# AV of both heads of a pair in one step of 32 matmuls over two PSUM banks, the heads alternating matmul by matmul

## Chip, cores, metric

One core of one Trainium2 chip. The metric is the device time of one launch in microseconds. A profiled run also has a span, from its first to its last instruction, about 2 us shorter. Every run called fast here is of the usual state; the two single looks are of state "unknown" (one run each) and are used for their traces.

## The reference, cut to what matters

```
q, k, v: 8 batches x 12 heads x 448 x 64
scores = (q/|q|) @ (k/|k|).T / tau;  attn = softmax(scores);  o = attn @ v      # AV
x = o as 3584 x 768;  out = ((x @ w1) * (x @ w2)) @ w3 @ w_out                  # the FFN
```

The kernel takes heads in 48 pairs. For a pair: normalise q and k (GpSimd, VectorE), transpose them (L308), scores (L326), exp (ScalarE), AV (L340), divide by the row sums (VectorE, "normalisation"), transpose back (L362). Six pairs make a batch; only then can the FFN matmuls of that batch run (L375, groups of 6 x 189 ns or 8 x 162 ns).

## The kernel before: the parts that matter

AV has one step per head. A group of four matmuls (c = 0..3) adds into 65 columns, 64 of v and one of ones, whose column is the row sum:

```python
def av(pp, hh):
    ps = full(f"av{pp}.{hh}")[:, :NJ * (D + 1)].rearrange("p (m d) -> p m d", m=NJ)   # one bank
    for m, q0 in enumerate(QT):
        for c in range(NJ):
            nc.tensor.matmul(ps[:, m, :], exps[pp][:, c, hh, q0:q0 + 128],   # weights
                             vt[:, 2 * i + hh, c, :],                        # moving, 65 columns
                             start=(c == 0), stop=(c == NJ - 1))
v_tiles = [wpool.tile([P, GH, NJ, D + 1], BF16, ...)]                        # rows of 130 bytes
```

The order of all instructions is not written down; a planner inside the kernel makes it when the program is built. It holds a book of when each engine is free and each bank is given back, from durations that it is told. TensorE takes the step of lowest rank among those that can start within 0.15 us of the earliest; attention comes before the FFN.

```python
HOP = 0.25                                             # from one engine to another
tol = 0.15 if eng == "PE" else 0.05
add(f"sc{nb}", ...)                                    # 3 chunks: needs all six banks 0..5
add(f"av{p}.{h}", [("PE", 0.525)], ..., banks=SHORT)   # any one of banks 0..5
add(f"an{p}.{h}", [("DVE", 0.62)], ..., [f"av{p}.{h}"], reads=[(f"av{p}.{h}", None)])  # gives it back
fill(f"a{b}.{fo}", 1.137, ...)                         # an FFN group, banks 7, 6, ...
```

What the planner makes is fixed on the chip: every engine works in that order and waits where something is late.

## Time and profile before

| | before |
|---|---|
| time, median of 2 | 393.09 us (392.95 to 393.23) |
| TensorE busy in the 298 us from 45 to 343 | 297.83 us |
| one AV block of 32, from its first start to the next instruction's | 1,029 ns |
| AV of the last pair starts | 341.3 us |
| after the last transposes back: FFN alone | 43 us |

How to read it: TensorE is busy without a gap, so the number of its nanoseconds is the time. The last row is the cushion of FFN work that attention can be late by; the prediction works out what of it is free. Starts are taken from the single records of the trace; the profile merges them.

### The profile page before, as it was taken

How to read it: one execution, taken by the hardware profiler on the slowest of the kernel's cores; microseconds unless marked ns; L12 is line 12 of the kernel's file. 1: busy time of each engine (PE TensorE's matmuls, PEld its weight loads, DVE VectorE, ACT ScalarE, POOL GpSimd, SP SyncE). 2: the span in 40 equal slices, each digit the busy share in tenths (PEclk: the TensorE clock that was granted, in tenths of full speed). 3: DMA queues.
4: the chain of work that ended last, by engine and by line, in shares of the span. 5: the costliest groups of instructions: out<-in, count | busy, mean ns of one | idle time of the engine just before them, and what ended most of it. 6: DMA issues, size and time to landing. Idle time of an engine off the chain costs nothing.

```text
span 391.0 us, 9650 instructions
## 1 busy us (share of the span) xinstructions
PE 382.9 (98%) x4012; PEld 231.1 (59%) x4012; DVE 215.5 (55%) x495; ACT 243.9 (62%) x401; POOL 243.8 (62%) x256
## 2 busy tenths in 40 slices
PE   8899999999999999999999999999999999999995
PEld 4578665565655666565655565555656566555553
DVE  5798745686737668557568657543534434330210
ACT  4998768456765766766765767746566666613222
POOL 8598998999999989999999999713400000000000
PEclk9999999999999999999999999999999999999999
DMA  8999999627476484828437194301200032004005
GB/s 142 199 203 200 210 208 195 82 35 134 96 91 86 79 149 80 108 32 145 85 45 103 26 143 105 35 2 42 82 2 3 3 88 75 2 2 121 0 10 153
DMA packets 43691, 35.18 MB, mean 90 GB/s; under 512 B 3968, under 2 KB 37632, under 8 KB 43648
## 3 DMA queue, kind: packets, MB, share of 16 engines
q0 software_dynamic: 38368, 23.11, 42.8%
q1 hardware_dynamic: 4784, 11.07, 9.7%
q8 instruction: 31, 0.51, 0.5%
q10 hardware_dynamic: 496, 0.40, 0.3%
q14 instruction: 12, 0.10, 0.1%
HBM read 46.66 MB, written 11.01 MB: 148 GB/s over the span
## 4 chain that ended last, share of the span: by engine, by line
PE 69%; POOL 21%; DMA 5%; issue 3%; DVE 1%; POOLq 0%; DVEq 0%
PE ps L375 47%; POOL nrm L289 9%; PE ps L340 9%; POOL sq L255 8%; PE ps L326 7%; DMA wo_sb<-in_moe_w_out_dram 4%; PE ps L308 3%; PE ps L362 2%; POOL raw L224 2%; POOL v_sb L240 2%; DMA raw<-in_k_dram 2%; DVE nrm L289 1%; DVE osd L353 0%; PE ps L388 0%; POOL vraw L231 0%
## 5 line engine op out<-in xcount | busy, mean ns | idle before, releaser
L331 ACT ACTIVATE expT<-ps 112x896 bf16<-112x896 f32 x192 | 166.1, 922 | 24.8 <-PE ps L326 24.6
L375 PE MATMUL ps<-xT,w_sb 128*128 128x448 bf16 x768 | 161.2, 353 | 0.0
L375 PEld LDWEIGHTS <-w_sb 128*128 128x128 bf16 x768 | 69.1, 98 | 66.1 <-issue 13.0
L289 POOL TENSOR_TENSOR nrm<-raw,rn 112x512 bf16<-112x512 bf16 x88 | 89.0, 1037 | 11.3 <-PE ps L308 10.0
L255 POOL TENSOR_TENSOR sq<-raw 112x512 bf16<-112x512 bf16 x85 | 86.0, 1040 | 0.7 <-DMA raw<-in_q_dram 0.5
L375 PE MATMUL ps<-w_sb,abT 128*128 128x384 bf16 (+2 forms) x456 | 80.0, 323 | 0.0
L421 DVE TENSOR_TENSOR abT<-a_sb,ps 128x448 bf16<-128x448 bf16 x64 | 39.7, 620 | 67.3 <-PE ps L375 64.3
L410 ACT CAST a_sb<-ps 128x448 bf16<-128x448 f32 x64 | 34.1, 534 | 58.3 <-PE ps L375 58.3
L261 DVE TENSOR_REDUCE ss<-sq 112x8 f32<-112x512 bf16 x96 | 62.9, 679 | 12.3 <-POOL sq L255 11.9
L375 PEld LDWEIGHTS <-abT 128*128 128x128 bf16 x456 | 41.7, 98 | 31.5 <-issue 7.0
L340 PEld LDWEIGHTS <-expT 112*128 112x128 bf16 x1536 | 54.9, 98 | 6.7 <-issue 1.0
L340 PE MATMUL ps<-v_sb,expT 112*128 112x65 bf16 x1536 | 57.7, 194 | 0.2 <-ACT expT L331 0.2
L326 PE MATMUL ps<-qkT 64*128 64x448 bf16 x384 | 48.5, 353 | 0.2 <-DVE osd L353 0.2
L381 ACT COPY out_sb<-ps 128x384 f32<-128x384 f32 (+1 forms) x43 | 20.5, 477 | 43.7 <-PE ps L375 40.4
L353 DVE TENSOR_TENSOR osd<-ps,rs 128x256 bf16<-128x256 f32 x96 | 40.8, 425 | 3.3
L316 DVE COPY qkT<-ps 128x896 bf16<-128x896 bf16 x48 | 29.6, 618 | 9.9 <-PE ps L308 9.9
L369 DVE COPY xT<-ps 128x448 bf16<-128x448 bf16 x48 | 18.6, 387 | 28.5 <-PE ps L362 23.1
L240 POOL COPY v_sb<-vraw 112x1536 bf16<-112x1536 bf16 x16 | 23.4, 1462 | 15.4 <-PE ps L340 12.0
L326 PEld LDWEIGHTS <-qkT 64*128 64x128 bf16 x384 | 13.4, 94 | 27.0 <-issue 20.7
L308 PE MATMUL ps<-ident,nrm 112*128 112x112 bf16 x384 | 26.9, 213 | 0.6 <-ACT expT L331 0.3
L383 DVE COPY out_sb<-ps 128x384 f32<-128x384 f32 (+1 forms) x14 | 7.5, 538 | 33.9 <-PE ps L375 33.9
L375 PE MATMUL ps<-wo_sb,w3t_sb 128*128 128x192 bf16 (+1 forms) x192 | 23.8, 273 | 1.2 <-DMA wo_sb<-in_moe_w_out_dram 1.2
(38 smaller groups left out, 208.8 us busy)
## 6 DMA issues: line engine op xcount, KB each, us to landing
vraw<-in_v_dram POOLq DMA_DIRECT2D x16, 336.0 KB, 5.6
raw<-in_q_dram POOLq DMA_DIRECT2D x15, 336.0 KB, 5.7
raw<-in_k_dram POOLq DMA_DIRECT2D x15, 336.0 KB, 7.6
w_sb<-in_moe_w_dram POOLq DMA_DIRECT2D x2, 1536.0 KB, 24.8
out_dram<-out_sb SPq DMA_DIRECT2D x7, 336.0 KB, 3.7
out_dram<-out_sb SPq DMA_DIRECT2D x8, 288.0 KB, 3.2
out_dram<-out_sb SPq DMA_DIRECT2D x8, 240.0 KB, 2.6
w_sb<-in_moe_w_dram POOLq DMA_DIRECT2D x3, 512.0 KB, 15.4
```

Of the source, the lines that this page charges most:

```text
L240: nc.gpsimd.tensor_copy(v_tiles[g % NV][:, :, :, :D], vraws.pop(g))
L255: eng.tensor_mul(o, x, x)
L261: nc.vector.reduce_sum(sss[g][:, t, 2 * i:2 * i + 2, :], sqs.pop((g, i, t)), axis=AX.X)
L289: eng.tensor_mul(nrms[g][:, i, t].rearrange("p j h d -> p h j d"), raw_of(g, t, i), rns[g][:, t, 2 * i:2 * i + 2].to_broadcast([P, 2, NJ, D]))
L308: nc.tensor.transpose(ps[:, 1 - t, j * P:(j + 1) * P], n[:, i, t, j].rearrange("p h d -> p (h d)"), ident[:P, :P])
L326: nc.tensor.matmul(sc[:, hh, :S], kq[:, c * P:c * P + 128], kq[:, S:], start=True, stop=True)
L331: nc.scalar.activation(exps[pp][:, c], scs.pop((pp, c))[:P, :, :S], ACT.Exp, scale=1.0 / float(tau))
L340: nc.tensor.matmul(ps[:, m, :], exps[pp][:, c, hh, q0:q0 + 128], vt[:, 2 * i + hh, c, :], start=(c == 0), stop=(c == NJ - 1))
L353: nc.vector.tensor_mul(osds[pp][:, :, hh, :], ps[:, :, :D], rs.to_broadcast([128, NJ, D]))
L375: nc.tensor.matmul(o, l, r, start=(i == 0), stop=(i == len(pairs) - 1))
L410: nc.scalar.copy(a_sbs[b, fo], pms.pop(("a", b, fo))[:, :S])
L421: nc.vector.tensor_mul(abts[b // 2][:, fo, c0:c0 + S], a_sbs.pop((b, fo)), pms.pop(("b", b, fo))[:, :S])
```

## The change

Its intent: matmuls that follow each other no longer add into the same bank. For that each head has a bank of its own, and the two steps become one.

```diff
-    def av(pp, hh):
+    def av(pp):
-        ps = full(f"av{pp}.{hh}")[...]
+        ps = [ps_all[:, b, :NJ * (D + 1)]... for b in plan.bank[f"av{pp}"]]
         for m, q0 in enumerate(QT):
             for c in range(NJ):
-                nc.tensor.matmul(ps[:, m, :], exps[pp][:, c, hh, ...], vt[:, 2 * i + hh, c, :], ...)
+                for hh in range(2):
+                    nc.tensor.matmul(ps[hh][:, m, :], exps[pp][:, c, hh, ...], vt[:, 2 * i + hh, c, :], ...)
...
+        add(f"av{p}", [("PE", 1.05)], ..., banks=[(n, n + 1) for n in range(0, 6, 2)])
         for h in range(2):
-            add(f"av{p}.{h}", [("PE", 0.525)], ..., banks=SHORT)
-            add(f"an{p}.{h}", [("DVE", 0.62)], ..., [f"av{p}.{h}"], reads=[(f"av{p}.{h}", None)])
+            add(f"an{p}.{h}", [("DVE", 0.62)], ..., [f"av{p}"], reads=[(f"av{p}", slice(h, h + 1))])
```

More of the change, by code (lines that the diff above doesn't have):

```diff
@@ L332, in exp @@
                              scale=1.0 / float(tau))
-    def av(pp, hh):
+    def av(pp):
         g, i = divmod(pp, GP)
         vt = v_tiles[g % NV]
-        ps = full(f"av{pp}.{hh}")[:, :NJ * (D + 1)].rearrange("p (m d) -> p m d", m=NJ)
+        ps = [ps_all[:, b, :NJ * (D + 1)].rearrange("p (m d) -> p m d", m=NJ)
+              for b in plan.bank[f"av{pp}"]]
         for m, q0 in enumerate(QT):
             for c in range(NJ):
-                nc.tensor.matmul(
-                    ps[:, m, :],
-                    exps[pp][:, c, hh, q0:q0 + 128],
-                    vt[:, 2 * i + hh, c, :],
-                    start=(c == 0), stop=(c == NJ - 1))
-        if hh == 0:
-            osds[pp] = head_pool.tile([128, NJ, 2, D], BF16, tag="osd", name="osd")
-        pav[pp, hh] = ps
+                for hh in range(2):
+                    nc.tensor.matmul(
+                        ps[hh][:, m, :],
+                        exps[pp][:, c, hh, q0:q0 + 128],
+                        vt[:, 2 * i + hh, c, :],
+                        start=(c == 0), stop=(c == NJ - 1))
+        osds[pp] = head_pool.tile([128, NJ, 2, D], BF16, tag="osd", name="osd")
+        for hh in range(2):
+            pav[pp, hh] = ps[hh]
     def av_norm(pp, hh):
@@ L621 @@
             reads=[(f"tr{p}", None)])
+        add(f"av{p}", [("PE", 1.05)], p, lambda e, p=p: av(p),
+            [f"exp{p}.{c}" for c in range(NJ)] + [f"spread{g}"] + ([f"av{p - 1}"] if last else []),
+            [("osd", ("osd", p))], [("exp", p), ("vt", g)],
+            banks=[(n, n + 1) for n in range(0, 6, 2)])
         for h in range(2):
-            add(f"av{p}.{h}", [("PE", 0.525)], p + 0.5 * h, lambda e, p=p, h=h: av(p, h),
-                [f"exp{p}.{c}" for c in range(NJ)] + [f"spread{g}"]
-                + ([f"av{p}.0"] if h else [f"av{p - 1}.1"] if last else []),
-                [] if h else [("osd", ("osd", p))], [("exp", p), ("vt", g)], banks=SHORT)
             add(f"an{p}.{h}", [("DVE", 0.62)], p + 0.5 * h - 0.5,
-                lambda e, p=p, h=h: av_norm(p, h), [f"av{p}.{h}"], reads=[(f"av{p}.{h}", None)])
+                lambda e, p=p, h=h: av_norm(p, h), [f"av{p}"],
+                reads=[(f"av{p}", slice(h, h + 1))])
         add(f"tb{p}", [("PE", 0.235)], p + 1, lambda e, p=p: trback(p),
```

## The prediction

> **What bounds the kernel now.** I read the page first: the busy row, the slices, the chain that ended last, and the rows of matmuls.
>
> ```profile
> PE 382.9 (98%) x4012; PEld 231.1 (59%) x4012; DVE 215.5 (55%) x495; ACT 243.9 (62%) x401; POOL 243.8 (62%) x256
> ...
> PE   8899999999999999999999999999999999999995
> ...
> POOL 8598998999999989999999999713400000000000
> PEclk9999999999999999999999999999999999999999
> ...
> L375 PE MATMUL ps<-xT,w_sb 128*128 128x448 bf16 x768 | 161.2, 353 | 0.0
> ...
> L340 PEld LDWEIGHTS <-expT 112*128 112x128 bf16 x1536 | 54.9, 98 | 6.7 <-issue 1.0
> L340 PE MATMUL ps<-v_sb,expT 112*128 112x65 bf16 x1536 | 57.7, 194 | 0.2 <-ACT expT L331 0.2
> ```
>
> TensorE has no gap from the third slice on, at full clock. L340 is AV. Its mean of 194 ns is a latency, not a cost: matmuls overlap, so the cost is the distance from one start to the next. To be sure that busy means moving, I then read the waits of TensorE alone:
>
> ```profile
> PE ps L475 <- DVE warm_sb L469: 1.3, 1, 1.3
> PE ps L375 <- DMA wo_sb<-in_moe_w_out_dram: 1.2, 2, 0.9
> PE ps L388 <- DMA w_sb<-in_moe_w_dram: 0.7, 1, 0.7
> PE ps L308 <- ACT expT L331: 0.3, 1, 0.3
> PE ps L308 <- DVE nrm L289: 0.3, 1, 0.3
> PE ps L326 <- DVE osd L353: 0.2, 1, 0.2
> PE ps L340 <- ACT expT L331: 0.2, 1, 0.2
> ```
>
> In all 4.2 us, nearly all in the first 45. The chain of waits goes through GpSimd from about 110 to 200 us, but it joins TensorE over one 0.2 us wait (L326), and the order of times shows why that is no second bound: the last normalised q and k of pair 20 ends at 120.9 us and its transposes start at 142.8, 22 us later; for pair 8 the lead is 4 us, for pair 41 53 us. So after some 80 us GpSimd is ahead, and what is saved on TensorE shows in the end, as long as it has something to do. Last, the order of time around one AV step:
>
> ```profile
> 227.65 0.39 PE L362 MATMUL ps<-ident,osd 128*128 128x128 bf16 x4
> 227.81 1.11 PEld L340 LDWEIGHTS <-expT 112*128 112x128 bf16 x32
> ...
> 227.87 1.19 PE L340 MATMUL ps<-v_sb,expT 112*128 112x65 bf16 x32
> ...
> 228.83 0.42 DVE L353 TENSOR_TENSOR osd<-ps,rs 128x256 bf16<-128x256 f32 x1
> ...
> 228.90 0.56 PE L308 MATMUL ps<-ident,nrm 112*128 112x112 bf16 x8
> ```
>
> Both heads already run as one block of 32 (46 of the 48 pairs do), from 227.87 to the next start at 228.90: 1.03 us. Head 0 is normalised while head 1 is still multiplied. So grouping two steps into one gains nothing by itself; what is new is the order inside.
>
> **What the skill says.** The Trainium skill, "TensorE: Matmul & The Clock Gate", section "Back-to-back issue gap", gives N/2.4 + 2.5 ns between starts at full clock. The trace agrees for long matmuls: 448 columns 189 ns (186.7 + 2.5), 112 columns 49 ns (49.2), 128 columns 56 ns (55.8). For AV's 65 columns it gives 29.6 ns; the trace has mostly 32 to 34. No page says what an accumulation into just-written elements costs. "PSUM — Partial Sum Buffer", section "The four PSUM rules", says that each bank is a separate SRAM and that two accumulation groups open at once in one bank cannot both start with the clearing flag; so heads that alternate need two banks, as the change has it. Its section "PSUM bank collisions raise a hardware error" forbids VectorE to read a bank that TensorE is writing: so neither head can be normalised before the last of the 32. No run tests that here; the kernel's semaphores keep it. "Perfetto Trace Analysis", section "Identifying the Most-Contended Engine", warns that matmul busy time is no measure of the roofline; the 353 ns of a matmul that starts every 189 ns is that.
>
> **The stall that the change aims at.** From the start times of the single records of the 46 whole AV blocks I took the mean distance at each place. Matmuls 0 to 15 are head 0 (m = 0..3, c = 0..3 inside), 16 to 31 head 1:
>
> after 0: 33.9, then 33.0, 32.6, 32.5;
> after 4: 29.1, then 33.5, 32.6, 32.5;
> after 8: 29.2, then 32.8, 32.5, 32.6; after 12: 29.2, then 33.7, 32.4, 32.7;
> after 16: 32.4, then 32.7, 32.4, 33.1; after 20, 24 and 28: 29.1 to 29.2, then the same as above.
>
> The sum of 31 is 996 ns, and with the step to the next instruction 1,029. The short distances follow a matmul that starts a new group in the bank; every matmul that adds to what the one before it wrote is followed by one of about 32.6. The plain reading: adding to elements written 29 ns ago isn't possible, some 32.5 ns must lie between. At 112 columns and more the matmul itself is longer than that, which is why L375 shows nothing. Two things disturb this reading. After 0 it is 34 mostly, but exactly 29 in all 7 blocks that follow transposes of 112 rows, so that is the change of rows (128 to 112). And matmul 16 starts a group in another bank, yet 32.4 follows it. I can't explain 16 by accumulation. Either going from one bank to another costs the same 3.4 ns when the matmuls are this short, or it is something of the moving operand (matmul 16 reads v just behind what 15 read, as do all the slow ones; 4, 8 and so on jump back).
>
> **The change part by part.**
> 1. Removed: nothing. 1536 matmuls and weight loads, the same shapes, 96 normalisations of two instructions, as before.
> 2. Order: consecutive matmuls never add to the same elements; the distance to the one before last is at least 58 ns. If the stall is the read of just-written elements (or of adjacent v), all distances become about 29.2: 32 x 29.2 = 934 against 1,029, so 95 ns a pair, 48 x 95 = 4.6 us. I take 85% of it (3.9 us) as falling where TensorE is the bound: the pairs up to the seventh or so run before 60 us, where waits on exp and weights can swallow it.
> 3. Normalisation: it starts after all 32. In the block above, VectorE ended head 1 at 229.81 (0.43 after 229.38), 0.91 us after AV's end. Now two heads follow the end, each 0.18 + 0.42 = about 0.57 us apart, so some 0.5 us later. This sits on the loop AV, normalise, free banks, next scores, since scores of 3 chunks need all six banks 0 to 5. It delays attention by up to 0.5 us a pair (24 us in all), but puts other matmuls (L375) in TensorE's stream in place of them. After the last transposes back (343.67 us) there are 43 us of L375 left; those that need the last pair are 16 groups of 1.13 us and some 10 us of output, 28 in all. So about 15 us of delay is free. Cost on the path: I put 0.2 us.
> 4. Banks: AV waits for an aligned free pair, not for any bank. Same cushion later; at the start (6 pairs, two-chunk scores, transfers not there yet) a worse fit can cost. The choices of engine fixed by name in the kernel were found for the old order. I put +0.5 us, 2 either way.
>
> Sum: -3.9 + 0.2 + 0.5 = -3.2 us: 389.9.
>
> **The rivals.**
> A: bank switching costs as much as accumulating. For: matmul 16. Against: the first matmul after 112-row transposes, surely in another bank, is followed by 29. Then all 32 distances are 32.5, the six short ones of each pair are lost: 48 x 6 x 3.4 = +1.0 us, and with 3 and 4 about 394.8. I give it 0.27.
> B: the order unties. Later normalisation slows attention by more than its cushion of 15 us, L375 runs out of inputs and TensorE gaps appear. For: the loop through six banks. Against: TensorE has L375 work in every stretch and ends with 43 us of it. Then 395 to 400. 0.08.
> C: the gain is there but absorbed: TensorE comes earlier to waits for ACT's exp, which ends 0.1 to 0.6 us before AV starts in most pairs. Against: an AV faster by 0.1 us moves the next scores, and so exp, forward too. Then 391.5 to 393. 0.15.
> D: weight loads bind at 32.5. Against: loads are of one form and follow at 29 after 4, 8, 12 as well. Then 393.7; within A's chance.
>
> **Range and chances.** The main case, 0.5 of the weight, lies at 388.3 to 391; C and A fill up to 395. The range is 387.8 to 395.2. Faster by 2% needs 385.2, 7.9 us, more than the 4.6 of all stalls: only a luckier order at the start gives that, 0.03. Slower by 2% is 401, B at its worst: 0.03.
>
> **What would show it.** Step 2: L340's starts within a block, 0.93 us for 32 in the chain or the order of time in place of 1.03; if 1.04, A was right. Step 3: the second normalisation ends about 1.4 us after AV's end, and TensorE waits for VectorE (L326 on osd) don't grow above 1 us. Step 4: the sum of TensorE waits before 60 us against 4.2. B: fewer than 35 us of L375 at the end, and gaps in the last slices. The prediction fails if distances don't change, or if 0.93 us shows and the span doesn't follow.

## The result, and the profile after

The changed kernel takes **402.25 us** (401.99 and 402.5): 1.0239 of before, 95% interval 1.0214 to 1.0264. It is slower, outside the range. Ratios here are the mean time of one kernel's fast runs over that of the other's in the same rounds, so not quite the ratio of the medians that stand beside them.

The page of the changed kernel (AV is L342 now, the FFN L377, normalisation L354 and L355, transposes back L364):

```profile
PE 384.8 (96%) x4012; PEld 231.3 (58%) x4012; DVE 214.3 (53%) x488; ACT 244.9 (61%) x405; POOL 246.3 (61%) x259
...
PE   8989999998879999999899999999999999999995
...
PEclk9989999999999999999999999999999999999999
...
L342 PE MATMUL ps<-v_sb,expT 112*128 112x65 bf16 x1536 | 55.7, 194 | 0.8 <-ACT expT L331 0.7
L326 PE MATMUL ps<-qkT 64*128 64x448 bf16 x384 | 49.7, 353 | 2.1 <-DVE osd L355 1.8
```

AV did get cheaper: 55.7 us busy against 57.7. From the starts, a block of 32 takes 979 ns against 1,029. But the row of slices, 10 us each, has holes between 90 and 120 us and just before 200, where before had none. Busy time of the engines by stretch, first before, then after (start and end; length; TensorE busy and count; then the other engines):

```profile
0.00:45.00 45.00, 41.01 (x513) 28.81 (x514) 35.99 (x79) 35.19 (x65) 36.15 (x48) 1.00 1.24 189
45.00:343.00 298.00, 297.83 (x3244) 177.60 (x3242) 171.27 (x402) 196.29 (x311) 207.69 (x209) 1.00 0.48 80
```

```profile
0.00:45.00 45.00, 40.75 (x470) 29.03 (x472) 32.46 (x69) 31.00 (x60) 37.56 (x50) 0.96 1.25 190
45.00:343.00 298.00, 290.51 (x3130) 171.45 (x3127) 167.00 (x385) 192.65 (x311) 208.69 (x210) 1.00 0.48 80
```

In the middle TensorE stood idle for 7.5 us (298 - 290.5), where before it was 0.2, and did 114 matmuls less. Whom TensorE waited for in the changed kernel:

```profile
PE ps L364 <- ACT expT L331: 2.7, 4, 0.7
PE ps L377 <- DVE abT L423: 2.1, 1, 2.1
PE ps L326 <- DVE osd L355: 1.8, 5, 0.9
PE ps L308 <- ACT expT L331: 1.4, 1, 1.4
PE ps L377 <- DVE w3t_sb L385: 1.3, 2, 0.8
PE ps L477 <- DVE warm_sb L471: 1.3, 1, 1.3
PE ps L342 <- ACT expT L331: 0.7, 2, 0.5
```

The first row, four waits of transposes back for exp, is at the ends of batches. One of them in order of time (start, length, engine, what; in brackets the idle time before it):

```profile
150.04 0.74 PE L326 MATMUL ps<-qkT 64*128 64x448 bf16 x6
151.49 0.38 PE L364 MATMUL ps<-ident,osd 128*128 128x128 bf16 x4 [0.71 <-ACT expT L331]
151.71 0.56 PE L308 MATMUL ps<-ident,nrm 112*128 112x112 bf16 x8
152.30 1.14 PE L342 MATMUL ps<-v_sb,expT 112*128 112x65 bf16 x32
```

No FFN matmul stands between: the saved-up FFN work has run out, and attention is the only thing left to do until the batch is complete. The count says so: at these four waits 16, 32, 48 and 80 FFN groups of six matmuls have run, and a batch has 16. Some 4.9 of the 7.5 us lie in such stretches. The second row is something else: at 116 us VectorE stood behind a sum that waited for GpSimd, so that an AV that had ended at 113.7 us was normalised only from 117.0 on, and an FFN group of TensorE waited 2.1 us for VectorE.

Attention has fallen behind: AV of pair 47 starts at 362.7 us in place of 341.3, 21.4 us later, and after the last transposes back only 29.9 us of FFN are left in place of 43.

Why attention is later is seen between one AV and the next scores. Before (TensorE and VectorE around pair 34):

```profile
254.00 1.19 PE L340 MATMUL ps<-v_sb,expT 112*128 112x65 bf16 x32
...
254.81 0.18 DVE L352 RECIPROCAL rs<-ps 128x4 f32<-128x4 f32 x1
...
255.04 1.30 PE L375 MATMUL ps<-xT,w_sb 128*128 128x448 bf16 x6
...
255.57 0.42 DVE L353 TENSOR_TENSOR osd<-ps,rs 128x256 bf16<-128x256 f32 x1
...
256.27 0.55 PE L326 MATMUL ps<-qkT 64*128 64x448 bf16 x4
```

After (pair 30):

```profile
241.58 1.14 PE L342 MATMUL ps<-v_sb,expT 112*128 112x65 bf16 x32
...
242.56 2.44 PE L377 MATMUL ps<-xT,w_sb 128*128 128x448 bf16 x12
242.79 0.18 DVE L354 RECIPROCAL rs<-ps 128x4 f32<-128x4 f32 x1 [0.25 <-PE ps L342]
...
243.56 0.42 DVE L355 TENSOR_TENSOR osd<-ps,rs 128x256 bf16<-128x256 f32 x1
...
244.93 0.55 PE L326 MATMUL ps<-qkT 64*128 64x448 bf16 x4
```

Before, the first normalisation starts before the block has ended, the second ends at 255.99, and one FFN group of six fits before the scores. After, the first starts behind the block, the second ends at 243.98, and two groups stand before the scores. In pairs 9 to 46 of the trace one group stands there in 26 of 38 cases before, in 3 of 38 after.

**The theory** that I took to the chip: both heads' banks come free some 0.5 us later; that passes the end of one FFN group, so the planner sets a second, and scores lose not 0.5 but a whole group; attention falls behind until the FFN work runs out at the ends of batches. **Rivals**: the pair of banks or the alternation itself costs; or the old order was lucky and any other costs as much. And for AV's own gain: is the stall that it removes one of accumulation, or of the moving operand?

### The profile page after: what moved, and what is told of

Same layout as the page of the kernel before. It is cut to its first block, busy times and chain, and to the rows that moved or that the text cites. A ratio compares the mean times of both kernels' runs of the same rounds, so it can differ in the third digit from the quotient of the medians.

```text
span 400.7 us, 9646 instructions
## 1 busy us (share of the span) xinstructions
PE 384.8 (96%) x4012; PEld 231.3 (58%) x4012; DVE 214.3 (53%) x488; ACT 244.9 (61%) x405; POOL 246.3 (61%) x259
## 4 chain that ended last, share of the span: by engine, by line
PE 64%; POOL 24%; issue 5%; DMA 3%; ACT 2%; DVE 2%; POOLq 0%; DVEq 0%; ACTq 0%
PE ps L377 43%; POOL sq L255 9%; POOL nrm L289 9%; PE ps L342 8%; PE ps L326 7%; DMA raw<-in_q_dram 3%; PE ps L308 3%; POOL raw L224 2%; POOL v_sb L240 2%; PE ps L364 2%; ACT expT L331 2%; POOL vraw L231 1%; DVE nrm L289 0%; POOL w_sb L243 0%; DVE osd L355 0%
## 5 line engine op out<-in xcount | busy, mean ns | idle before, releaser
L377 PE MATMUL ps<-xT,w_sb 128*128 128x448 bf16 x768 | 158.7, 353 | 2.1 <-DVE abT L423 2.1
L377 PEld LDWEIGHTS <-w_sb 128*128 128x128 bf16 x768 | 69.8, 98 | 71.4 <-issue 15.3
L289 POOL TENSOR_TENSOR nrm<-raw,rn 112x512 bf16<-112x512 bf16 x90 | 90.9, 1037 | 17.6 <-ACT expT L331 7.5
L377 PE MATMUL ps<-w_sb,abT 128*128 128x384 bf16 (+2 forms) x456 | 79.4, 323 | 0.0
L377 PEld LDWEIGHTS <-abT 128*128 128x128 bf16 x456 | 41.7, 98 | 30.0 <-issue 5.9
L342 PEld LDWEIGHTS <-expT 112*128 112x128 bf16 x1536 | 53.0, 98 | 6.8 <-issue 1.5
L342 PE MATMUL ps<-v_sb,expT 112*128 112x65 bf16 x1536 | 55.7, 194 | 0.8 <-ACT expT L331 0.7
L326 PE MATMUL ps<-qkT 64*128 64x448 bf16 x384 | 49.7, 353 | 2.1 <-DVE osd L355 1.8
L383 ACT COPY out_sb<-ps 128x384 f32<-128x384 f32 (+1 forms) x45 | 21.4, 476 | 41.8 <-PE ps L377 39.6
L355 DVE TENSOR_TENSOR osd<-ps,rs 128x256 bf16<-128x256 f32 x96 | 40.8, 425 | 3.5 <-DVE rs L354 0.2
L354 DVE RECIPROCAL rs<-ps 128x4 f32<-128x4 f32 x96 | 17.0, 177 | 33.4 <-PE ps L342 32.8
L377 PE MATMUL ps<-wo_sb,w3t_sb 128*128 128x192 bf16 (+1 forms) x192 | 24.3, 278 | 1.3 <-DVE w3t_sb L385 1.3
```

Of the source, the lines that this page charges most:

```text
L289: eng.tensor_mul(nrms[g][:, i, t].rearrange("p j h d -> p h j d"), raw_of(g, t, i), rns[g][:, t, 2 * i:2 * i + 2].to_broadcast([P, 2, NJ, D]))
L326: nc.tensor.matmul(sc[:, hh, :S], kq[:, c * P:c * P + 128], kq[:, S:], start=True, stop=True)
L342: nc.tensor.matmul(ps[hh][:, m, :], exps[pp][:, c, hh, q0:q0 + 128], vt[:, 2 * i + hh, c, :], start=(c == 0), stop=(c == NJ - 1))
L355: nc.vector.tensor_mul(osds[pp][:, :, hh, :], ps[:, :, :D], rs.to_broadcast([128, NJ, D]))
L377: nc.tensor.matmul(o, l, r, start=(i == 0), stop=(i == len(pairs) - 1))
```

## The experiments

All 16 kernels of the experiments gave correct results. "Ready" is the mean time from AV's last start until both heads are normalised, "one group" the pairs of 38 with a single FFN group before the next scores, both from pairs 9 to 46; "idle" is 298 us less TensorE's busy time between 45 and 343 us.

| run | median us | ratio | AV block ns | ready us | one group | idle us |
|---|---|---|---|---|---|---|
| before | 393.09 | | 1,029 | 1.05 | 26 | 0.2 |
| changed | 402.25 | 1.024 | 979 | 1.70 | 3 | 7.5 |
| e1 old order, heads alternate | 396.71 | 1.011 | 980 | 1.42 | 26 | 1.1 |
| e2 changed, heads in turn | 403.79 | 1.029 | 1,028 | 1.23 | 3 | 6.1 |
| e3 before, late normalisation | 403.03 | 1.029 | 1,029 | 1.15 | 3 | 6.1 |
| e4 before, other c order | 391.48 | 0.998 | 979 | 1.11 | 26 | 0.8 |
| f1 before, v rows 192 bytes | 391.51 | 0.997 | 973 | 1.12 | 26 | 1.0 |
| f2 before, v rows 132 bytes (one look) | 394.51 | | 1,021 | 1.05 | 26 | |
| f3 changed, one normalisation | 395.35 | 1.008 | 979 | 1.44 | 11 | 3.0 |
| f4 changed, any two banks (one look) | 401.09 | | 979 | 1.65 | 3 | 8.4 |
| g1 changed, AV told 0.98 | 400.04 | 1.018 | 980 | 1.64 | 1 | 6.5 |
| g2 f1, AV told 0.49 | 395.43 | 1.006 | 974 | 1.08 | 17 | 2.2 |
| g3 f1, AV told 0.50 | 392.88 | 1.000 | 974 | 1.15 | 17 | 1.7 |
| g4 before, normalisation told 0.66 | 399.69 | 1.017 | 1,029 | 1.08 | 10 | 3.1 |
| h1 changed, told 0.39 | 396.66 | 1.010 | 980 | 1.58 | 28 | 2.1 |
| h2 f3, told 0.74 | 394.39 | 1.003 | 981 | 1.37 | 30 | 2.2 |
| h3 f1, told 0.58 | 392.02 | 0.998 | 974 | 1.09 | 27 | 0.8 |
| h4 before, told 0.60 | 398.28 | 1.013 | 1,028 | 1.07 | 23 | 2.6 |

The kernel before took 392.3 to 393.0 us in the rounds of each set. Each set e, f, g and h ran beside it on one chip; e and g had the same chip, f and h two others.

### What the stall inside AV is

**e4: another c order.** Everything else as before.

```diff
-            for c in range(NJ):
+            for c in (0, 2, 1, 3):
```

> The kernel before with AV's inner order c = 0, 2, 1, 3: every matmul still adds to what the one before it wrote, but no matmul reads the v that lies just behind what the one before it read, except at the change of head. Theory RAW (adding to just-written elements needs 32.5 ns): distances stay at 32 to 34 with 29 after matmuls 4, 8, 12, 20, 24, 28; time same as before within 0.3%. Rival V (neighbouring v is what stalls): distances near 29 everywhere but after 16, 390 to 391 us.

The block fell to 979 ns though each matmul still adds to what the one before it wrote. The median distances are 29 ns after 1, 2, 3 and most others, and 33 after 16, where alone v is still read on from where it ended. So the stall was not accumulation: it was v. The alternation of the change helps for the same reason, because head 1's v lies 520 bytes away. The time gained is 0.24% (interval 0.02 to 0.47%), half a microsecond less than rival V foretold.

**f1: v's rows 192 bytes apart**, and **f2: 132 bytes apart**; order, banks and instructions of before.

```diff
-    v_tiles = [wpool.tile([P, GH, NJ, D + 1], BF16, ...)]
+    v_tiles = [wpool.tile([P, GH, NJ, 96], BF16, ...)]        # f2: 66
...
-                    vt[:, 2 * i + hh, c, :],
+                    vt[:, 2 * i + hh, c, :D + 1],
```

> The kernel before, every instruction in its place and AV in the order c = 0 to 3, heads in turn; only v's rows of 65 elements (130 bytes) lie 192 bytes apart, so that no two slices share or adjoin a 64-byte stretch. After the run with another c order, theory V (a moving operand that begins in the stretch of memory where the one before it ended stalls): 29 ns after all matmuls but for a rest of some 4 to 6 ns once in four, block 935 to 980 ns, time 390 to 391.7 us, 0.2 to 0.6% under before. Theory RAW (adding to just-written elements) is all but dead; if it lived, the pattern of before with 1,029 ns and 392.3 us.

> As the run with rows 192 bytes apart, but with 132 bytes: slices still share 64-byte stretches, only they no longer touch (2 bytes between) and all begin at a multiple of 4 bytes. If shared stretches stall: 1,029 ns a block as before. If it is the odd start or touching: 935 to 980 ns.

With 192 bytes the plain old order gives 973 ns. The line of AV in f1, against 57.7 us before:

```profile
L340 PE MATMUL ps<-v_sb,expT 112*128 112x65 bf16 x1536 | 55.1, 193 | 0.2 <-ACT expT L331 0.2
```

With 132 bytes the pattern of before is back at 1,021 ns, except that 29.2 now follows matmul 16 too. So touching is not needed; a gap of 2 bytes doesn't help. One reading fits all four layouts: a moving operand stalls by some 3.4 ns when it begins in the same 16 bytes in which the one before it ended. Rows of 130 bytes do so at all steps forward; rows of 132 do except between the heads, where 4 x 132 = 528 is a multiple of 16. That takes the tile itself to begin at a multiple of 16, which no run shows, so the 16 is argued, not shown. In all the faster blocks a stall of 4 to 6 ns is left about once in four or five matmuls; what it is stays open.

f1 is the version that beats both kernels: 0.9967 of before (0.9949 to 0.9985). That is clear of the noise, but well under the 2% at which a verdict says faster, and e4 with 0.9976 can't be told from it. Of the 48 x 56 ns = 2.7 us saved in AV about half shows in the time: a part came back, as in a wait of 0.69 us before 177.6 us, where an FFN output group now comes before its input is ready.

### Where the loss of the change comes from

**e2: the changed kernel with the heads in turn.** Order on every engine and banks are exactly those of the changed kernel.

```diff
-        for m, q0 in enumerate(QT):
-            for c in range(NJ):
-                for hh in range(2):
+        for hh in range(2):
+            for m, q0 in enumerate(QT):
+                for c in range(NJ):
```

> The changed kernel with its one AV step, its pairs of banks and exactly its order on all engines, but inside the step head 0's 16 matmuls come first and head 1's after. Theory O: the alternation has nothing to do with the loss, time 402 to 405 us (up to 48 x 0.05 = 2.4 us more than the changed kernel's 402.3), with 29 ns only after each fourth matmul again. Rival R (alternating banks costs something outside the block, as on the clock or in VectorE's reads): it falls back towards 393 to 396 us.

403.79 us, and idle 6.1: the loss stays without the alternation. It stays too though head 0 can be normalised early again (ready 1.23 in place of 1.70). So in this order it isn't the chip's lateness that costs; the order does.

**e3: the kernel before, only head 0's normalisation waits for head 1's AV in the planner's book.** Two steps, single banks.

```diff
-                lambda e, p=p, h=h: av_norm(p, h), [f"av{p}.{h}"], reads=...
+                lambda e, p=p, h=h: av_norm(p, h), [f"av{p}.{h}", f"av{p}.1"], reads=...
```

> The kernel before, two AV steps of 16 in single banks, the heads one after the other; only head 0's normalisation is made to wait for head 1's AV too, and the planner is told so. Theory N (late normalisation alone makes the loss, by way of the plan): 400 to 404 us, scores after two groups of L375 in place of one in most pairs, gaps of TensorE at the ends of batches. Rival P (what costs is the one step in an aligned pair of banks): 393 to 395 us.

403.03 us (the four runs lie between 400.65 and 405.13), 3 of 38, idle 6.1 (298 - 291.90):

```profile
45.00:343.00 298.00, 291.90 (x3124) 173.63 (x3122) 166.60 (x387) 187.88 (x304) 208.07 (x209) 0.99 0.48 80
```

Telling the planner of the late normalisation alone makes the whole loss. Neither the one step nor the pair of banks is needed. Nor is lateness on the chip: the first reciprocal of a pair starts 0.21 us before AV's last matmul at the median, against 0.20 in the kernel before and 0.27 after it in the changed one.

**f4: any two of six banks** in the changed kernel.

```diff
-            banks=[(n, n + 1) for n in range(0, 6, 2)])
+            banks=[(m, n) for n in range(6) for m in range(n)])
```

> The changed kernel, whose AV may take any two of the six banks in place of an aligned pair. The planner then makes the same order on all engines, only with other banks for 13 pairs. Theory N: one look at 401 to 404 us. Rival P (the aligned pair is what costs): below 398 us.

401.09 us in one look, with the same order and idle 8.4: the aligned pair is not the cause.

**e1: the order of before, with the heads alternating.** Where the old plan has both AV steps side by side (46 pairs), the first writes out nothing and the second all 32 matmuls.

```diff
+        heads = (hh,)
+        if pp in together:
+            if hh == 0:
+                return
+            heads = (0, 1)
...
+                for h in heads:
```

> The heads alternate, but every instruction stands where the kernel before has it: where its plan has the two AV steps of a pair side by side (46 of 48), they are written out as one block of 32 with the heads alternating, in the two single banks that the old plan chose. Theory O (the time is lost by the order that the planner makes when it is told of late normalisation): the AV block stays at 979 ns as in the changed kernel instead of 1,029, the order costs nothing, so 46 x 0.05 = 2.3 us less than before: 390.3 to 391.5 us. Rival L (it is lost on the chip, whatever the order, because both heads' banks come free later): TensorE waits for the normalisation before scores, 396 to 403 us.

396.71 us, so at the lower edge of the rival's range and 5 us above mine. A fast block in the old order is not free: VectorE now waits for AV in nearly every pair (the waits of e1's VectorE; before these were 7.0 us in 10 waits),

```profile
DVE rs L361 <- PE ps L348: 26.3, 44, 1.8
```

and scores, which the old order sets behind one FFN group, come before the banks are free. Pair 34's step on TensorE and, of VectorE, the end of its normalisation:

```profile
257.99 0.91 PE L326 MATMUL ps<-qkT 64*128 64x448 bf16 x6
258.83 0.93 PE L384 MATMUL ps<-xT,w_sb 128*128 128x448 bf16 x4
```

```profile
257.70 0.42 DVE L362 TENSOR_TENSOR osd<-ps,rs 128x256 bf16<-128x256 f32 x1
```

The six score matmuls hold TensorE for 0.84 us (258.83 - 257.99), against the usual 0.67. Summed over the blocks, TensorE spends 46.5 us on scores and what they wait for, against 44.1, and AV, which now needs head 1's bank at its second matmul, another 2.0 us of waits. That is more than the 2.3 us that AV saves, though not all of the 4.4 us by which e1 is slower. So both are true: late banks cost some 5 us as waits when the order ignores them, and 8 to 10 when the planner makes room for them.

**f3: both heads in one normalisation**, in the changed kernel: one reciprocal and one multiplication over the two banks, and the planner told 0.95 us in place of 2 x 0.62.

```diff
-            add(f"an{p}.{h}", [("DVE", 0.62)], ...)       # twice
+        add(f"an{p}", [("DVE", 0.95)], ...)
```

> The changed kernel, but VectorE normalises both heads in one reciprocal and one multiplication over the pair of banks, and the planner is told 0.95 us in place of 2 x 0.62. Theory N (the loss grows with the time from AV's end to the free banks): both heads ready about 1.3 us after AV's end in place of 1.7, scores after one group of L375 more often, time 394 to 398 us. Rival P (the one step in a pair of banks itself): stays at 401 to 403 us.

```profile
L357 DVE TENSOR_TENSOR osd<-ps,rs 128x512 bf16<-128x512 f32 x48 | 33.2, 692 | 1.7
...
L356 DVE RECIPROCAL rs<-ps 128x8 f32<-128x8 f32 x48 | 9.9, 205 | 21.2 <-PE ps L342 18.9 <-ACT expT L331 1.1 <-ACT rt L273 0.9
```

692 + 205 ns in place of 2 x (425 + 177): ready after 1.44 us, 11 pairs with one group, 395.35 us. A shorter way from AV to free banks takes back some 6 of the 9 us (ratio 1.008 in place of 1.024), with the same matmuls.

**g1: the changed kernel, AV told 0.98 us**, its true length.

```diff
-        add(f"av{p}", [("PE", 1.05)], ...
+        add(f"av{p}", [("PE", 0.98)], ...
```

> The changed kernel with one number altered: the planner is told 0.98 us for the AV step, which is what the block of 32 takes on the chip, in place of 1.05. Theory N (late normalisation makes the loss): only the smaller part comes back, 397 to 400.5 us. Rival M (the planner was told a wrong time, and that is the loss): 389 to 394 us.

400.04: about 2 us come back, in the expected range. A wrong number for AV is not the cause.

### Is it lateness, or just another order?

**g4: the kernel before, normalisation told 0.66 us in place of 0.62.** The instructions stay as they are.

```diff
-            add(f"an{p}.{h}", [("DVE", 0.62)], ...
+            add(f"an{p}.{h}", [("DVE", 0.66)], ...        # h4: 0.60
```

> The kernel before with nothing altered but a number: the planner is told 0.66 us for each normalisation in place of 0.62. The instructions and their dependences are those of before, the order is another. Theory N: an order drawn anew without late normalisation costs little, 393 to 396.5 us. Rival Q (the old order was a lucky find, and any other costs what the change costs): 399 us or more.

399.69 us: the rival's hit. The book of the planner says why it might not be chance. Counted from AV's end it has head 0 normalised at -0.525 + 0.25 + x, head 1 at x later, the banks free 0.25 after that: 2x - 0.025. One FFN group takes 1.137 and the tolerance is 0.15, so scores come next if 2x - 0.025 is at most 1.287. With x = 0.62 it is 1.215; with 0.66 it is 1.295, 8 ns too much. In the trace one group stands in 10 pairs in place of 26. For the changed kernel it is 0.25 + 2x + 0.25 = 1.74: far too much.

The planner needs no chip, so this can be tested without one. It was run alone on the kernels here. Its own book (an estimate by the planner, no measurement) ends at 393.3 us for the kernel before, 399.4 for the changed one, 399.5 for e3 and 396.2 for g4. With other x in the kernel before, the book ends at 393 to 395 us with one group in 16 to 27 pairs for all twelve values tried from 0.56 to 0.656, and at 396 to 405 us with one group in at most 11 pairs for the five tried from 0.66 to 0.75. The changed kernel steps up between 0.39 (391.3) and 0.45 (398.2). So the step lies where the sum above puts it, and some 6 of the 9 us stood in the book before the chip was asked.

But a part of g4's loss is made at the start, and not in the book:

```profile
32.88 0.36 PE L308 MATMUL ps<-ident,nrm 112*128 112x112 bf16 x4
35.53 0.37 PE L308 MATMUL ps<-ident,nrm 112*128 112x112 bf16 x4 [2.29 <-DVE nrm L289]
```

This single wait at 33 us is for normalised q and k (nrm): one multiplication of VectorE took 2.99 us, where in the kernel before the one at that place, 32.69 us, took 0.68, and GpSimd was multiplying during 2.45 us of it. h4 and g2 have the same (3.31 and 3.34 us, 2.7 and 2.6 us beside GpSimd). That the overlap is the cause no run tests. The wait is not one for AV's normalisation, and 3.4 us at half clock follow it. How much that is can be read from the starts: for each matmul, the distance to the next start less the usual one of its shape, summed up. Against the kernel before, TensorE loses 2.5 us in the first 45 us and 4.4 us after. To tell the two apart I ran four more orders, all on the near side of the threshold.

**h1: the changed kernel told 0.39** (0.25 + 0.78 + 0.25 = 1.28), and **h2: f3 told 0.74** (1.24).

```diff
-            add(f"an{p}.{h}", [("DVE", 0.62)], ...        # h2: add(f"an{p}", [("DVE", 0.95)], ...
+            add(f"an{p}.{h}", [("DVE", 0.39)], ...        # h2: add(f"an{p}", [("DVE", 0.74)], ...
```

> The changed kernel, with the planner told 0.39 us in place of 0.62 for each of the two normalisations, so that by its book scores fit behind one group of L375 again (0.25 + 0.78 + 0.25 = 1.28, under 1.287). On the chip both heads are still ready only some 1.45 us after AV's last start, so TensorE waits a few tenths before many scores. Theory T: 394 to 398 us, as for the alternation in the old order (396.7). Rival Q (any other order than the old one costs the same): 399 us or more.

> The changed kernel with both heads normalised in one reciprocal and one multiplication, and the planner told 0.74 us for it in place of 0.95 (0.25 + 0.74 + 0.25 = 1.24, under 1.287; on the chip both heads are ready 1.23 us after AV's last start). Theory T: one group of L375 before most scores, short waits, 391 to 394.5 us, at or near the kernel before. Rival Q: 397 us or more.

h1: 396.66 us, one group in 28 pairs, idle 2.1: the changed program, told a shorter time than is true, wins 5.6 us, and lands where e1 did. h2: 394.39, 30 pairs. Both are within the theory's range.

**h3: f1 told 0.58** and **h4: before told 0.60** (diffs as for g4).

> The kernel before with v's rows 192 bytes apart and the planner told 0.58 us for each normalisation in place of 0.62: more room under the threshold. Theory T: 389 to 392 us, perhaps the best of all. Rival Q: 395 us or more.

> The kernel before with nothing altered but the planner told 0.60 us in place of 0.62: the sister of the run told 0.66, an order drawn anew, but on the near side of the threshold. Theory T: 391.5 to 395.5 us. Rival Q: as the one told 0.66, 397 us or more.

h3 ends at the edge of its range (392.02). h4 misses: 398.28 us, though 23 pairs have one group. Its trace has the same kind of wait as g4's, 2.2 us before 36.3 us, and one of 1.2 us before 21.6, where before had 0.3. But by the starts only 1.8 us are lost in the first 45 us and 3.9 us after. The planner's book for h4 ends at 392.9 us, so this loss isn't one that the planner foresaw; what costs the 3.9 us stays open. So an order drawn anew can cost 5 us by itself.

**g2 and g3: f1 told 0.49 and 0.50 for AV.**

```diff
-            add(f"av{p}.{h}", [("PE", 0.525)], ...
+            add(f"av{p}.{h}", [("PE", 0.49)], ...         # g3: 0.5
```

> The kernel before with v's rows 192 bytes apart, and the planner told 0.49 us for each AV step in place of 0.525, so that the order fits the faster block. If the part of the AV gain that was given back at waits is a matter of the order: 389 to 391 us, under the 391.5 of the same kernel with the old order. If not: 391 to 393.

> As the run told 0.49, but 0.50: another draw of the order with the same instructions. 389 to 391.5 us; how far it lies from its neighbour shows how much an order is worth by chance.

Both missed: 395.43 and 392.88 us, no better than f1 with the old order. Telling the planner the truth about AV gains nothing; g2 again lost 2.3 us at 33 us.

What is left of the rival: the total time of a new order is in part a draw, worth up to some 7 us. The part from 45 us on still tells the kernels apart: idle is 6.1 to 8.4 us in all five kernels whose planner is told of two late normalisations (changed, e2, e3, f4, g1), and 0.2 to 3.1 in the twelve others of the table that have a figure. By the starts, which count hidden waits too, the five lose 8.6 to 10.4 us there against the kernel before, and the others at most 5.9 (h1). Two limits: changed, e2 and f4 have one and the same order on TensorE, so the five are three orders. And the five kernels with a new order but without two late normalisations in a row (g2, g3, g4, h3, h4) lose 1.8 to 4.4 us there, those that keep the old order and its normalisation (e4, f1, f2) at most 1.1. So the old order was a good one, and some 2 to 4 of the change's 10 us may be no more than the loss of it; the rest is what late normalisation brings.

## Why the prediction was wrong, point by point

- **The bound** (TensorE without gaps, GpSimd far ahead): right. It is also why every gap counted.
- **Step 1**, the same instructions: right.
- **Step 2**, AV's distances: the direction right, the size half. 979 ns in place of the 934 foretold: 50 ns a pair, 2.4 us in all and not 4.6, because a stall of 4 to 6 ns about once in four is left. The "plain reading", that adding to just-written elements needs 32.5 ns, was wrong (e4, f1). Matmul 16, which I named as what it couldn't explain, was the fact to follow; the third explanation beside it, the v just behind, was right. (The prediction's "exactly 29 in all 7 blocks" is a small slip: the trace has 6 such blocks, five with 29 and one with 30.) Rival A (bank switching, 0.27) falls with it, and D too.
- **Step 3** is the one that failed: "So about 15 us of delay is free. Cost on the path: I put 0.2 us." The lateness itself was foreseen well (1.4 us after AV's end; the trace has 1.43 at the median, counted from the next instruction's start as the prediction did). That its sum ("up to 0.5 us a pair (24 us in all)") lies near the 21.4 us by which the last AV came later is luck: attention is delayed by whole groups in some pairs, not by 0.5 us in each. The book-keeping of the cushion was wrong. It exists only at the end of the kernel; an FFN group of a batch can't run before attention has finished that batch, so work saved up for the end doesn't fill a gap at 100 us. The FFN work ran out at the ends of batches, and most of the 7.5 us of idle TensorE are the result, where I had 0.2 us for the whole step. A second fault, first in the chain: 0.5 us of lateness doesn't cost 0.5 us, it costs the next whole FFN group when the planner finds the banks not free at the end of the first.
- **Step 4**, "+0.5 us, 2 either way": the banks cost nothing (f4). The draw of an order is worth more than I allowed (g4, h4: 5 to 7 us), and I had noted that choices were "found for the old order" without drawing the consequence. The prediction makes no use of the planner's own book for the new step, which ends 6 us later.
- **The sum**: AV -2.4; idle between 45 and 343 us +7.3; the difference to the measured 9.2 is +4.3, shorter waits hidden under the matmuls' recorded lengths, and the start. By the starts it is +1.6 us before 45 us and +10.3 after, which with -2.4 gives the 9.5 us between the last matmuls of the two traces. Both splits are readings of the traces, and no run isolates them.
- **Rival B** was the answer and had 0.08. Its sign came as written: 29.9 us of FFN at the end, under 35. Its gaps came earlier than "the last slices", and its 395 to 400 us were still too low. C did not happen.

## What to carry to other kernels

When a merged step lets go of its buffers later, follow the loop that waits for them and ask what unit of filler stands in it: half a microsecond late can cost a whole filler group, and a cushion helps only where its work may run. A static order made from told durations is in part a draw. Where a program makes the order, run it with the new numbers before the chip, and compare variants with the order held fixed (as e1, e2 and f1 do) before an effect is put down to the instructions. And if one record contradicts the plain reading of a stall, try the cheapest edit that separates the readings: here a permuted loop of four and a padded row gave the gain of the change without its cost.

## What the Trainium skill lacked or had wrong

- "TensorE: Matmul & The Clock Gate", section "Back-to-back issue gap": its formula for the isolated gap at full clock, N/2.4 + 2.5, comes to 29.6 ns for 65 columns (an estimate from the page), whatever the operands' addresses. The runs show 32.2 ns a matmul (1,029 / 32) when v's slices of 130 bytes are read one behind the other, and 30.4 (973 / 32) when they lie 192 bytes apart. No page says that the place of the moving operand behind the previous one matters; the pages that speak of SBUF's 16-byte cachelines don't have this cost.
- The same section says that in a stream where each matmul follows a weight load of its own the formula under-counts at small N, with 81 ns measured for 128 columns. Here every matmul has its own load (4,012 of each), and those of 128 columns start every 56 ns, as the formula has it.
- The same page, section "What's actually happening": its table has the clock at half after at least one idle window of some 3.4 us. Here single gaps of 1.4 us (the changed kernel, up to 21.4 us) and 2.3 us (g4, up to 35.5 us) were followed by half clock for 3.41 us, in the changed kernel from 22.3 us (the last three figures below are granted clock, transfer share and GB/s), and in e3 half clock came at 102.0 us with no gap over 0.8 us in the 80 us before. Gaps of the same length in other runs (1.5 us in e4, 2.2 us in h4) were not followed by it.

```profile
22.30:25.70 3.40, 3.40 (x45) 3.33 (x44) 2.77 (x9) 2.33 (x7) 3.03 (x5) 0.50 1.25 204
25.70:29.10 3.40, 3.40 (x39) 2.33 (x37) 2.53 (x6) 2.81 (x6) 3.39 (x4) 1.00 1.22 207
```
